# SSM tap angles as wrapping 32-bit integers on GpSimd, with sine and cosine read from integers, in a gated S4D and feed-forward kernel

## The chip, the cores and the metric

The kernel runs on one core of one Trainium2 chip. The metric is the device time of one execution in microseconds; 619.15 us is the median of two runs of the kernel before. In the profile the engines are PE (TensorE; PEld is its weight load), DVE (VectorE), ACT (ScalarE), POOL (GpSimd) and SP (SyncE, which issues the transfers).

## What is computed

An S4D state-space convolution over L = 2048 positions and D = 640 channels with N = 128 modes a channel, and a feed-forward layer with 1728 hidden units, both on tokens of the same shape, mixed by a gate:

```python
dt = jnp.exp(log_dt)
A = -jnp.exp(log_A_real) + 1j * A_imag
C = (C_real + 1j * C_imag) * dt[:, None]
P = jnp.exp((A * dt[:, None])[:, :, None] * pos[None, None, :])
K = 2.0 * jnp.einsum("dn,dnl->dl", C, P).real
...
y = jnp.fft.irfft(Uf * Kf[None, :, :], L2)[:, :, :L]
...
return g * a + (1 - g) * b
```

What matters here is `K`: for each channel 2048 taps, each a sum over 128 modes of an exponential times a cosine. The kernel writes a position as 32 times a coarse step (64 of them, numbered by `slots()`) plus a fine step (32 of them). By the addition theorem the taps of a channel are then a product of matrices over the modes: fine factors (128 x 32) against coarse factors (128 x 64). Each factor is a magnitude (exponential) times a sine or a cosine of an angle counted in turns.

## The kernel before

All of `f32` is multiplied on PE in the form `F32R`, large operands split in a high and a low part. The work has three strands.

*Feed-forward.* Three passes over the hidden units (`PARTS`), each over eight groups of 256 tokens. PE's products go to the tile `pf`: 512 columns for the first layer, 320 for the second. In the program this is the queue `ff`, with the best rank.

*Taps.* 40 steps of 16 channels; two steps make a pair. `params()` first turns the parameters, 128 channels by 640 on chip, into four quantities (the angle of a step `th`, the decay `la`, the start angle `ph`, the logarithm of the amplitude `mx`). `split` writes a high and a low part of each to memory (`ps`), and `load_rows` reads four steps of them back as `PS`, with one row for each of 16 channels, 4 quantities and 2 parts on the partitions. In each step `phases` multiplies these rows on PE by a constant, block-diagonal table `tg`: the result `pg` holds 1024 angles for each of 128 modes (16 channels, 32 fine and 32 coarse). ACT casts `pg` to whole turns (`cs`), DVE subtracts them (`sn`), and DVE clears the sign bit for the cosine (`cs`). `exponents` multiplies the same rows by other parts of `tg`: `px` (1024 coarse exponents) and `pe` (512 fine ones), and ACT takes `Exp` of both, into `mg` and `me`, and `Sin` of `sn` and `cs`. `factors` multiplies on DVE, in five instructions: `G` (two), `mg`, `cs`, `sn`. `taps` lets PE multiply the factors of a pair of steps into `pk` (128 small matmuls), DVE transposes `pk` into `kt`, POOL adds the skip term `dsk` to `kt`, and SP stores it (`kd`).

*Convolution.* When the last `kd` is under way, the taps' pools close and those of the convolution open (`start` in `conv`). Five blocks of 128 channels run through `stage1`, `stage2`, `inv2`, `relay` and `inv1`: PE's results go to `pc`, and DVE, ACT and POOL work on `ku`.

*Order.* `Plan` is a list scheduler that runs while the program is built. It has an estimate of each task's duration, a rank, and rings of buffers (`ring`), and gives each engine its instructions in one fixed order; on the chip each engine runs them in that order and waits on semaphores. A task that takes a slot of a ring waits until the users of an earlier tile are done. `taps` has a poorer rank on PE (`GTR`) than the feed-forward, so `pf` fills PE between the pairs; `phases` and `exponents` of a step are joined, so that `pg`, `px` and `pe` follow each other. All operations are recorded through one helper, so that one line number (L326) stands for all of them, and the tile names tell them apart.

Of the kernel before, what the change touches and what calls it, by code (L numbers as in the profile page):

```python
# [10 lines left out]
F32 = mybir.dt.float32  # L11
F32R = mybir.dt.float32r
# [7 lines left out]
NT = D // 128  # L20
# [46 lines left out]
TN = 0.7  # L67

# [10 lines left out]
def tables():  # L79
# [20 lines left out]
    tg = np.zeros((16, 8, 176))  # L100
    tg[:, :2, :32], tg[:, :2, 32:64], tg[:, 2:4, :32] = b, 32 * b + 16, 1
    tg[:, 4:6, 64:128], tg[:, 4:6, 128:160], tg[:, 6:, 128:160] = 32 * slots(), b, 1
    tg[np.arange(16), :, 160 + np.arange(16)] = 1
    f = lambda x: np.ascontiguousarray(x.astype(np.float32))
    return dict(t_g=f(tg.reshape(128, 176)), t_f1=f(np.tile(np.stack([f1, f1[slots()]], axis=1), (2, 1, 1))), t_w=f(w.reshape(128, 64)),
# [251 lines left out]
class Kernel:  # L357
    def __init__(self, tc, ctx, io, out):
# [7 lines left out]
        self.sc = dict(kd=T([NT, 4, 128, 16, 32], "kd"), ps=[T([1, 128, 8, 128], "ps0"), T([NT - 1, 128, 8, 128], "ps1")],  # L366
# [464 lines left out]
    def params(self):  # L831
# [5 lines left out]
        def step(eng, dur, fn, kb=0, ch='c', deps=()):  # L837
            last[ch] = [A(eng, 'prm' + ch, dur, fn, [*last[ch], *deps], kb=kb, rank=dict(a=PA, c=3, l=PL)[ch])]
            return last[ch][0]

        def start():
# [6 lines left out]
            for n in ("th", "ac", "as", "mx", "mn", "r", "s", "ph", "ra", "sa"):  # L848
                tl[n] = T(n)
            tl['ni'] = T("ni", I32)  # L850
        def start_c():
# [5 lines left out]
        last.update(a=[self.prm_load], c=[self.prm_load_c])  # L857

# [18 lines left out]
        self.rows_st = [], []  # L877

# [15 lines left out]
        split(0, 'th', 'a')  # L894
        steps(13, 0.68, lambda V: exp_(V, tl['la'], tl['ni'], tl['ra'], tl['sa']), 'a')
        ex = last['a']
        steps(NT, 0.2, scaled('la', 'la', -1.0), 'a')
        split(4, 'la', 'a')
# [35 lines left out]
        split(6, 'mx', 'l')  # L934
        for cond, two, turn in ((ALU.is_gt, True, 0.25), (ALU.is_lt, False, 0.5)):
# [8 lines left out]
        steps(3, 0.7, R(lambda V, ac, as_, cr, ci, mx, mn, r, s, ph, th, ni: (  # L944
            V.tensor_scalar(ni, th, 1008.0, None, op0=ALU.mult),
            V.scalar_tensor_tensor(r, th, 1008.0, ni, op0=ALU.mult, op1=ALU.subtract), V.tensor_add(ph, ph, r))), deps=ex)
        split(2, 'ph', 'c')
        done = [*last['a'], *last['c'], *last['l'], *self.rows_st[0], *self.rows_st[1]]
        self.tg_done = []


        def steps_in():
            tl['tgs'] = self.prm.tile([128, 176], F32, name="tgs")
            D_.dma_start(tl['tgs'], io['t_g'])

        def spread(ds):
            def go():
                a, b = self.tg[:, :2048].rearrange("p (x d j) -> p d x j", x=2, j=64), self.tg[:, 2048:].rearrange("p (d j) -> p d j", j=32)
                for d in ds:
                    m = tl['tgs'][:, 160 + d:161 + d]  # L960
                    S.mul(a[:, d], tl['tgs'][:, :128].rearrange("p (x j) -> p x j", x=2), m)
                    S.mul(b[:, d], tl['tgs'][:, 128:160], m)
            return go
        a = A('SP', 'tg', 0.62, steps_in, [self.prm0], kb=88, rank=TGR)
        if TGR > 5:
            self.late_loads.append(a)
        for d in range(0, 16, 2):
            self.tg_done.append(A('ACT', 'tg', 1.1, spread(range(d, d + 2)), [a], rank=TGA))
        return [*done, *self.tg_done]

    def ssm(self, C=16):
# [10 lines left out]
        self.tg = gk.tile([128, 2560], F32R, name="tg")  # L982
        dsk = gk.tile([128, n // 2, 2 * Q], F32, name="dsk")
        nc.gpsimd.memset(dsk, 0.0)
        for k, v in dict(pg=1, px=1, pk=1, sc=5, mg=4, G=2, kt=2, PS=2).items():
            ring(k, v)
# [18 lines left out]
        def load_rows(c):  # L1005
            r_ = tok('PS')

            def load():
                t = gk.tile([128, 4, 128], F32R, name="PS", bufs=2)
                src = self.sc['ps'][c >= 8][c // 8 - (c >= 8), c % 8 * C:c % 8 * C + 4 * C]  # L1010
                D_.dma_start(t.bitcast(F32), src.rearrange("(s p) k n -> (p k) s n", p=C))
                for k in range(4):
                    R[c + k] = t[:, k]
            a = A('SP', 'rows', 0.62, load, self.rows_st[c >= 8], take=[r_], kb=256, rank=1)
            for k in range(4):
                rows[c + k] = a, r_

        tasks, f = {}, {}
        I = lambda x: x.bitcast(I32)


        def phases(c):
            p_, s_ = tok('pg'), tok('sc')
            rd, r_ = rows[c]

            def pe():
                p = self.psg.tile([128, 4, 256], F32, name="pg")
                pf = p.rearrange("p d j -> p (d j)")
                st['pg'] = pf.rearrange("p (d j) -> p d j", j=64)
# [4 lines left out]
            def whole():  # L1034
                st['sc', c] = [st['gp'].tile([128, C, 64], F32, name=k, bufs=5) for k in ("sn", "cs")]
                S.copy(I(st['sc', c][1]), st['pg'])
# [474 lines left out]
```

## Time and profile before

| what | value |
|---|---|
| median of two runs | 619.15 us (617.43 to 620.88) |
| the profiled execution: span from first to last instruction | 615.6 us, 3.55 under the median |
| granted TensorE clock over the span | 1.000 |
| HBM | 67.79 MB read, 39.06 MB written |
| `pg` on PE, ACT, DVE (all matmuls, casts, subtractions) | 25.3, 40.4, 48.6 us busy |
| `px` on PE and ACT | 25.3, 41.2 us busy |
| table loads on ACT | 42, 53.9 us busy |

A row of a group reads: line, engine, operation, output and inputs by the program's names, shapes, count, then the busy time and the mean duration in ns, then the engine's idle time just before these instructions and who ended it. A row of a timeline or of the chain begins with its start and its duration in us. A row by stage has the stretch, its length, and for each engine the busy time and the number of instructions, then the granted clock, the share in which the DMA engines were busy, and GB/s. Matmuls are pipelined, so that their durations overlap; the distance between two starts is what one costs.

### The profile page before, as it was taken

To read this page: it belongs to the slowest core of one execution; us is meant where nothing else is said; L and a number is where in the kernel's file an instruction comes from. 1 tells how busy PE (TensorE), PEld (TensorE's weight loads), DVE (VectorE), ACT (ScalarE), POOL (GpSimd) and SP (SyncE) were. 2 spreads that over 40 slices of the span, in tenths; PEclk is the share of its full clock that TensorE was granted. 3 is DMA by queue.
4 is the path that set the end of the run, shared out by engine and by line. 5 is a ranking of instruction groups with operands and counts; after the bars stand their busy time and mean duration, and the time that the engine had idled before them with its cause. 6 is when DMAs were issued, how large, how long until landed. Compare 5 with 4: busy or idle time off the path is not lost.

```text
span 615.6 us, 18337 instructions
## 1 busy us (share of the span) xinstructions
PE 603.2 (98%) x7864; PEld 478.9 (78%) x7864; DVE 505.8 (82%) x794; ACT 399.2 (65%) x579; POOL 92.6 (15%) x134
## 2 busy tenths in 40 slices
PE   8999999999999999999999999999989999999996
PEld 6898988889879989989978988966565564755656
DVE  5998669999978999999999999866867796866942
ACT  6569269999898798887898989222235244352470
POOL 0000000000000000000000000002507062451744
PEclk9999999999999999999999999999999999999999
DMA  8993954624566435435331352768340836725244
GB/s 288 398 367 126 357 190 179 235 59 158 164 221 237 158 100 211 146 101 196 114 121 61 105 168 83 236 229 307 118 176 2 241 100 209 259 75 172 78 137 138
DMA packets 54474, 108.05 MB, mean 176 GB/s; under 512 B 5497, under 2 KB 30713, under 8 KB 53497
## 3 DMA queue, kind: packets, MB, share of 16 engines
q1 hardware_dynamic: 54168, 106.63, 51.1%
q8 instruction: 62, 1.02, 0.6%
q10 hardware_dynamic: 224, 0.25, 0.1%
q14 instruction: 20, 0.16, 0.1%
HBM read 67.79 MB, written 39.06 MB: 174 GB/s over the span
## 4 chain that ended last, share of the span: by engine, by line
PE 90%; DVE 3%; DMA 2%; ACT 2%; issue 1%; POOL 1%; ACTq 0%; DVEq 0%; POOLq 0%; SPq 0%
PE pf L326 59%; PE pc L326 18%; PE pk L326 6%; PE pg L326 3%; PE px L326 3%; PE pe L326 1%; DMA ws<-in_B_w_dram 1%; DVE G L326 1%; POOL q L326 1%; DVE ku L326 1%; DMA wq<-in_w_dram 1%; DMA kd<-kt 1%; DVE mg L326 0%; ACT L326 0%; DMA ws<-y__84 0%
## 5 line engine op out<-in xcount | busy, mean ns | idle before, releaser
L326 PE MATMUL pf<-xx,w1h 128*128 128x512 f32 x560 | 176.0, 402 | 1.2 <-DVE w1h L326 0.9
L326 PEld LDWEIGHTS pf<-xx,w1h 128*128 128x128 f32 x560 | 103.7, 190 | 36.6 <-issue 12.7
L326 PE MATMUL pf<-xx,w1l 128*128 128x512 f32 x260 | 102.2, 393 | 0.0
L326 ACT COPY ku<-pc 128x512 f32<-128x512 f32 (+1 forms) x60 | 44.1, 758 | 81.7 <-PE pc L326 55.9
L326 DVE STREAM_TRANSPOSE ku<-pc 128x512 f32<-128x512 f32 x80 | 50.4, 685 | 23.3 <-PE pc L326 23.2
L326 POOL TENSOR_TENSOR kt<-kt,dsk 128x8 f32<-128x8 f32 x20 | 9.0, 451 | 394.9 <-DVE kt L326 341.2
L326 POOL TENSOR_TENSOR ku<-ku 128x256 f32<-128x256 f32 x80 | 56.4, 742 | 69.5 <-DVE ku L326 49.3
L326 PE MATMUL pf<-w2h,hh 128*128 128x320 f32 x192 | 59.3, 313 | 0.8 <-DVE q L326 0.8
L326 PE MATMUL pf<-w2l,hwh 128*128 128x320 f32 x192 | 59.2, 309 | 0.0
L326 PE MATMUL pf<-w2h,hwh 128*128 128x320 f32 x192 | 59.1, 309 | 0.0
L326 PE MATMUL pf<-w2h,hwl 128*128 128x320 f32 x192 | 56.9, 310 | 1.8 <-DVE hwl L326 1.8
L326 PE MATMUL pf<-w2l,hh 128*128 128x320 f32 x192 | 58.5, 309 | 0.0
L326 PEld LDWEIGHTS pf<-xx,w1l 128*128 128x128 f32 x260 | 49.0, 189 | 10.9 <-DVE w1l L326 0.2
L326 DVE TENSOR_TENSOR ku<-pc,ku 128x512 f32<-128x512 f32 x80 | 52.5, 682 | 4.2 <-ACT ku L326 2.9
L326 ACT CAST cs<-pg 128x1024 int32<-128x1024 f32 x40 | 40.4, 1010 | 21.7 <-PE pg L326 21.4
L326 ACT ACT_TABLE_LOAD x42 | 53.9, 1283 | 0.8
L326 DVE TENSOR_TENSOR sn<-pg,cs 128x1024 f32<-128x1024 f32 x40 | 48.6, 1214 | 2.3 <-ACT cs L326 2.3
L326 DVE TENSOR_TENSOR mg<-mg,cs 128x1024 f32<-128x1024 f32 x40 | 48.9, 1221 | 1.7 <-ACT cs L326 0.2
L326 PE MATMUL pf<-w2h,hl 128*128 128x320 f32 x160 | 48.0, 316 | 0.0
L326 ACT ACTIVATE cs<-cs,half_pi 128x1024 f32<-128x1024 f32 x40 | 45.6, 1140 | 0.0
L326 PE MATMUL pc<-ku,tm 64*32 64x256 f32 x1280 | 42.6, 392 | 0.5 <-issue 0.2
L326 ACT ACTIVATE sn<-sn 128x1024 f32<-128x1024 f32 x40 | 42.2, 1055 | 0.2
(151 smaller groups left out, 1250.7 us busy)
## 6 DMA issues: line engine op xcount, KB each, us to landing
xx<-xt SPq DMA_DIRECT2D x24, 640.0 KB, 5.6
xt<-xx SPq DMA_DIRECT2D x16, 640.0 KB, 7.2
part<-q SPq DMA_DIRECT2D x16, 640.0 KB, 3.1
q<-part SPq DMA_DIRECT2D x16, 640.0 KB, 4.4
xl<-in_u_r_dram SPq DMA_DIRECT2D x16, 320.0 KB, 4.3
xu<-in_u_b_dram SPq DMA_DIRECT2D x5, 1024.0 KB, 6.2
kd<-kt SPq DMA_DIRECT2D x80, 64.0 KB, 1.8
xu<-in_x_t_dram SPq DMA_DIRECT2D x6, 640.0 KB, 6.0
```

Source lines behind the costliest of these rows:

```text
L326: self._last = self._tc.keep_in_program_order(f(*a, **k))
```

## The change

*Angles.* The angles are no longer products on PE. `params()` takes, on DVE, the fractions of a turn of 16 angles and of one angle of a step (`fraction`), transposes them, the decay and the start angle on PE (`across`: five 128x128 transposes each, into `tr`), and lets ACT write them, times 2^32, as 32-bit integers into `cn` (the decay stays f32). Four POOL instructions of 640 columns make the cosine's and the odd-multiple variants. `cn` goes to memory and comes back for four steps at a time as `cn`, with the modes on the partitions. In each step POOL makes `ca` (1024 integers: the counts of a channel times odd numbers), `ck` (512: the counts times 0 to 31) and `fa` (1024: `ck` plus the start angle); sums and products wrap at 32 bits, which takes away whole turns. ACT reads `ca` and `fa` as integers into `Sin` with the scale 2 pi / 2^32, in place.

*Exponents.* `px` is gone: DVE multiplies the decay in `cn` by a row of 64 slot numbers `td` into `mg`, and ACT takes `Exp` of it from SBUF. `pe` stays, one matmul, with half of the rows (two quantities) and a table `tg` of 1024 columns for two steps.

*Factors.* Four DVE instructions instead of five: the two fine products become one of 1024 columns, on `fa`.

*Around it.* `tg` is spread from its small form by two POOL instructions instead of 32 on ACT; of the splits two are left (decay, amplitude). The rings `pg`, `px` and `sc` go; `ca` (4 slots), `fa` (7) and `tm` (2, the buffer of `ck`) come. The first reading of `ck` by the convolution waits for the last angle step, since the buffer is shared.

```diff
+    odd = 2 * b + 1
+    ti = np.concatenate([odd, np.where(b % 2, -odd, odd), b, [1 << 30]]).astype(np.int32)
...
+        def across(k, src, ch, deps=()):
...
+                for t in range(NT):
+                    self.E.transpose(tl['tr', k][:, t], tl[src][:, t], self.ident)
...
+                if k == 5:
+                    S.copy(o.bitcast(F32), x)
+                else:
+                    S.mul(o, x, 2.0 ** 32)
...
+        def fraction(to, src, k, n='ni'):
...
+                V.tensor_scalar(i, x, k, None, op0=ALU.mult)
+                V.scalar_tensor_tensor(o, x, k, i, op0=ALU.mult, op1=ALU.subtract)
...
-                for h in range(2):
-                    x = slice(h * 512, h * 512 + 512)
-                    self.E.matmul(pf[:, x], R[c], self.tg[:, x], start=True, stop=True)
...
-                S.copy(I(st['sc', c][1]), st['pg'])
...
-            d = A('DVE', 'g1', 1.14, lambda: V.tensor_sub(st['sc', c][0], st['pg'], I(st['sc', c][1])), [b],
-                  use=[p_, s_], rank=G1R)
-            e = A('DVE', 'g1', 0.62, lambda: V.tensor_scalar(I(st['sc', c][1]), I(st['sc', c][0]), 0x7fffffff, None,
-                                                             op0=ALU.bitwise_and), [d], use=[s_], rank=G1R, port=True)
...
+            def coarse():
+                t = st['ca', c] = st['gp'].tile([128, C, 2, 32], F32, name="ca", bufs=CA)
+                P.tensor_tensor(t.bitcast(I32), two(0), self.ti[:, None, :64].rearrange("p o (s j) -> p o s j", s=2).to_broadcast([128, C, 2, 32]),
+                                op=ALU.mult)
...
+                P.tensor_tensor(st['tm', c], X[c][:, 4, :, None].to_broadcast([128, C, 32]),
+                                self.ti[:, None, 64:96].to_broadcast([128, C, 32]), op=ALU.mult)
...
+                P.tensor_tensor(t.bitcast(I32), st.pop(('tm', c))[:, :, None].to_broadcast([128, C, 2, 32]), two(2), op=ALU.add)
...
+                    S.activation(x, x.bitcast(I32), AF.Sin, scale=TWO_PI / 2 ** 32)
...
-                    self.E.matmul(pf[:, x], R[c], self.tg[:, 1024 + h * 512:1536 + h * 512], start=True, stop=True)
...
+                V.tensor_mul(t, X[c][:, 5, :, None].bitcast(F32).to_broadcast([128, C, 64]),
+                             self.td[:, None].to_broadcast([128, C, 64]))
...
-                    elif k == 3:
-                        V.tensor_mul(cs[:, :, :32], me, cs[:, :, :32])
                     else:
-                        (P if POOLED else V).tensor_mul(sn[:, :, :32], me, sn[:, :, :32])
+                        V.tensor_mul(st['fa', c], st['me', c][:, :, None].to_broadcast([128, C, 2, 32]), st['fa', c])
```

The order of the instructions moves with it. POOL in the tap stage, before: all of the skip sums of the 20 pairs stand in a row, with the convolution's first sums behind them.

```order
L326 TENSOR_TENSOR kt<-kt,dsk 128x8 x20
L326 TENSOR_TENSOR ku<-ku 128x256 x32
L326 TENSOR_TENSOR yo<-yo,yj 128x512
L326 TENSOR_TENSOR yo<-yo,yj 128x256
L326 TENSOR_TENSOR q<-q,ws 128x128 x2
```

After, a stretch of the same stage: the skip sum of a pair, then the angle instructions of the next two steps, and so on for all pairs.

```order
L329 TENSOR_TENSOR kt<-kt,dsk 128x8
L329 TENSOR_TENSOR ca<-cn,ti 128x1024
L329 TENSOR_TENSOR ck<-cn,ti 128x512
L329 TENSOR_TENSOR fa<-ck,cn 128x1024
L329 TENSOR_TENSOR ca<-cn,ti 128x1024
L329 TENSOR_TENSOR ck<-cn,ti 128x512
L329 TENSOR_TENSOR fa<-ck,cn 128x1024
L329 TENSOR_TENSOR kt<-kt,dsk 128x8
```

So POOL's stage of 20 small instructions becomes one of 140, and a skip sum stands behind the angles of two steps.

DVE in the same stage, before, for one step and the beginning of the next (`q` is the feed-forward's running sum, `xl` the gate's product):

```order
L326 TENSOR_TENSOR sn<-pg,cs 128x1024
L326 TENSOR_SCALAR cs<-sn 128x1024
L326 SCALAR_TENSOR_TENSOR G<-mg,sn 128x16x32
L326 TENSOR_TENSOR G<-mg,sn 128x16x32
L326 TENSOR_TENSOR mg<-mg,cs 128x1024
L326 TENSOR_TENSOR q<-pf,q 128x320
L326 TENSOR_TENSOR cs<-me,cs 128x16x32
L326 TENSOR_TENSOR sn<-me,sn 128x16x32
```

After, for a step:

```order
L329 STREAM_TRANSPOSE kt<-pk 128x8x2x32
L329 TENSOR_TENSOR mg<-cn,td 128x1024
L329 TENSOR_TENSOR q<-pf,q 128x320
L329 TENSOR_TENSOR mg<-cn,td 128x1024
L329 SCALAR_TENSOR_TENSOR G<-mg,ca 128x16x32
L329 TENSOR_TENSOR G<-mg,ca 128x16x32
L329 TENSOR_TENSOR mg<-mg,ca 128x1024
L329 TENSOR_TENSOR fa<-me,fa 128x1024
```

The pair of `sn` and `cs` with its input from PSUM (`pg`) is gone, and the product of the exponents stands ahead of the factors that use it.

PE at the end of the tap stage, before: behind the last `pk` the first matmuls of the convolution (`pc`) stand between matmuls of the feed-forward (`pf`).

```order
L326 MATMUL pk<-G,sn 32x64 x4
...
L326 MATMUL pc<-ck,tf 64x512 x8
L326 MATMUL pf<-xx,w1h_4198 128x512 x2
L326 MATMUL pf<-xx,w1l_4199 128x512
L326 MATMUL pc<-xu,tf 64x512 x12
L326 MATMUL pf<-xx,w1h_4225 128x512 x2
L326 MATMUL pf<-xx,w1l_4226 128x512
```

After, there are seven `pf` and then the convolution's first block without any:

```order
L329 MATMUL pk<-G,fa 32x64 x4
...
L329 MATMUL pf<-w2h_4211,w2l_5195 128x320
L329 MATMUL pc<-ck,tf 64x512 x8
L329 MATMUL pc<-xu,tf 64x512 x16
L329 MATMUL pc<-ck,tf 64x512 x8
L329 MATMUL pc<-ku,tm 32x256 x128
L329 MATMUL pc<-ck,tf 64x512 x4
```

Behind the last `pk` there were 156 `pf` of 512 columns and 288 of 320; now there are 60 and 127. The others have moved ahead of it, into the room that `pg` and `px` took.

More of the change, by code (lines that the diff above doesn't have):

```diff
@@ L942, in params @@
             V.tensor_scalar(mn, mn, -2.0, 1.0, op0=ALU.mult, op1=ALU.add), V.tensor_mul(ph, ph, mn))))
[L944 to L968, printed above, removed]
+        across(2, 'ph', 'c', deps=last['t'])
+        self.cn_st = []
+        for k, gs in enumerate((slice(0, 2), slice(2, 2 * NT))):
+            self.cn_st.append(A('SP', 'prm', 0.62, lambda k=k, gs=gs: D_.dma_start(self.sc['cn'][k].bitcast(I32), tl['cn'][:, gs]),
+                                list(turned), kb=196 * (gs.stop - gs.start), rank=1))
+        done = [*last['a'], *last['c'], *last['l'], *self.rows_st[0], *self.rows_st[1], *self.cn_st]
         return [*done, *self.tg_done]
@@ L1006, in load_rows @@
             r_ = tok('PS')
+            k = c >= 8
             def load():
[L1009 to L1019, printed above, removed]
-        def phases(c):
-            p_, s_ = tok('pg'), tok('sc')
+                t, x = gk.tile([128, 2, 128], F32R, name="PS", bufs=2), gk.tile([128, 6, 64], I32, name="cn", bufs=2)
+                src = self.sc['ps'][k][c // 8 - k, c % 8 * C:c % 8 * C + 4 * C]
+                D_.dma_start(t.bitcast(F32), src.rearrange("(s p) k n -> (p k) s n", p=2 * C))
+                D_.dma_start(x, self.sc['cn'][k].bitcast(I32)[:, c // 4 - 2 * k])
```

171 lines of the change are left out of this document (105 added, 66 removed).

## The prediction

> **What bounds the kernel now.** I read the page's busy shares first, then the busy time by stage, then the chain of waits, then the instruction groups of each engine in the middle stage, and last the POOL timeline set beside the DVE timeline. The first two views:
>
> ```profile
> span 615.6 us, 18337 instructions
> PE 603.2 (98%) x7864; PEld 478.9 (78%) x7864; DVE 505.8 (82%) x794; ACT 399.2 (65%) x579; POOL 92.6 (15%) x134
> ...
> core 0: us, PE busy (x) PEld busy (x) DVE busy (x) ACT busy (x) POOL busy (x), PEclk, DMA share, GB/s
> ...
> 84.20:404.20 320.00, 317.70 (x4042) 280.05 (x4040) 296.54 (x440) 271.49 (x317) 8.80 (x19) 1.00 0.45 150
> 404.20:615.60 211.40, 204.54 (x3408) 127.33 (x3404) 145.03 (x236) 78.27 (x161) 82.94 (x108) 1.00 0.49 161
> ```
>
> PE is busy for 98% of the span, so the sum of PE's work sets the end. But the middle stage, in which the taps are made, has DVE at 296.5 of 320 us and ACT at 271.5 too, while POOL does 8.8 us. The chain shows where that stage begins and ends:
>
> ```profile
> 84.67 1.01 ACT cs L326
> ...
> 402.30 1.92 PE pk L326 x128
> 404.22 4.30 PE pf L326 x18
> 408.52 1.88 PE pc L326 x16
> ```
>
> The convolution (`pc`) begins only behind the last `pk`: its pools open when the last taps are out. So there are two ways to lose or win: PE work saved, and the time at which the last `pk` can run. One step (16 channels, 40 of them) takes 320/40 = 8.0 us now.
>
> **PE, saved and added.** The rows of one visit, a group for a 128x128 f32 pass, and the first and last of a run of 29 matmuls of 320 columns:
>
> ```profile
> 136.46 0.62 PE L326 MATMUL pg<-tg,PS 128*128 128x512 f32 x2
> 136.92 0.62 PE L326 MATMUL px<-tg,PS 128*128 128x512 f32 x2
> 137.38 0.40 PE L326 MATMUL pe<-tg,PS 128*128 128x512 f32 x1
> ...
> L326 PE MATMUL pe<-ident 128*128 128x128 f32 x12 | 2.9, 434 | 1.5 <-POOL ident masks.py:199 1.5
> ...
> 145.00 0.30 PE L326 MATMUL pf<-w2h,hh 128*128 128x320 f32 x1
> ...
> 149.09 0.30 PE L326 MATMUL pf<-w2h,hh 128*128 128x320 f32 x1
> ```
>
> Starts are what count on a pipelined engine: four matmuls from 136.46 to 137.38 are 0.23 us each. The change removes the two of `pg` and the two of `px` in each step: 160 x 0.23 = 36.8 us of PE. It adds 20 transposes (4 of 5). Their price is not in the trace: by columns it would be 0.23/4 = 0.06, as two of the 0.24 us passes (2.9/12) it would be 0.48. I take 0.23 each, one such pass, the middle of ends that lie 8 us apart in all: 4.6 us, between 1.2 and 9.7. Net 32 us off PE.
>
> **DVE, for each step.** The groups of the middle stage:
>
> ```profile
> L326 DVE TENSOR_TENSOR mg<-mg,cs 128x1024 f32<-128x1024 f32 x40 | 48.9, 1221 | 1.7 <-ACT cs L326 0.2
> L326 DVE TENSOR_TENSOR sn<-pg,cs 128x1024 f32<-128x1024 f32 x40 | 48.6, 1214 | 2.3 <-ACT cs L326 2.3
> L326 DVE TENSOR_SCALAR cs<-sn 128x1024 int32<-128x1024 int32 x40 | 27.5, 687 | 0.9
> L326 DVE TENSOR_TENSOR G<-mg,sn 128x512 f32<-128x512 f32 x40 | 27.4, 684 | 0.0
> L326 DVE TENSOR_TENSOR sn<-me,sn 128x512 f32<-128x512 f32 x40 | 27.3, 682 | 0.0
> L326 DVE TENSOR_TENSOR cs<-me,cs 128x512 f32<-128x512 f32 x40 | 27.3, 682 | 0.0
> L326 DVE SCALAR_TENSOR_TENSOR G<-mg,sn 128x512 f32<-128x512 f32 x40 | 27.0, 675 | 4.0 <-ACT sn L326 4.0
> ...
> L326 DVE SCALAR_TENSOR_TENSOR xl<-xl,gw 128x640 f32<-128x640 f32 x14 | 11.5, 821 | 4.3 <-DMA xl<-in_u_r_dram 4.3
> ...
> L326 DVE TENSOR_TENSOR w1l<-ws,w1h 128x640 fp32r<-128x640 f32 x9 | 7.1, 812 | 0.0
> L326 DVE TENSOR_TENSOR w2l<-ws,w2h 128x640 fp32r<-128x640 f32 x9 | 7.1, 818 | 0.0
> ```
>
> A step costs 1.221 + 1.214 + 0.687 + 0.684 + 0.682 + 0.682 + 0.675 = 5.85 us now. Gone are the subtraction (1.214), the mask (0.687) and two products (1.364); new are `mg<-cn,td` and `fa<-me,fa`, both 1024 columns, 1.22 each by the `mg<-mg,cs` row. That leaves 1.22 x 3 + 0.684 + 0.675 = 5.02 us, 0.83 less. Alone, DVE would need 296.5 - 33 = 263.5 us for the stage, 6.6 a step. But every one of the five that are left reads two tensors from SBUF; the biggest one removed read one of its two from PSUM.
>
> **ACT.** It loses the cast, and its two sines stay two of 1024 columns, now read as int32. The rows show no price for that type, since the cast to int32 takes no longer than a sine in f32:
>
> ```profile
> L326 ACT ACTIVATE sn<-sn 128x1024 f32<-128x1024 f32 x40 | 42.2, 1055 | 0.2
> L326 ACT CAST cs<-pg 128x1024 int32<-128x1024 f32 x40 | 40.4, 1010 | 21.7 <-PE pg L326 21.4 <-ACT hwh L326 0.2
> ```
>
> So 1.01 us a step goes, and the 32 small spreads of `tg`. ACT has 48 us to spare in the stage already, so the gain is costed at nothing; if the cover went, 1.06 a sine would still fit into 8 us.
>
> **POOL, the new work.** The nearest rows are plain f32 sums:
>
> ```profile
> L326 POOL TENSOR_TENSOR ku<-ku 128x256 f32<-128x256 f32 x80 | 56.4, 742 | 69.5 <-DVE ku L326 49.3 <-issue 20.1
> L326 POOL TENSOR_TENSOR yo<-yo,yj 128x512 f32<-128x512 f32 x8 | 10.1, 1282 | 15.3 <-ACT yo L326 15.3
> ```
>
> The slope is (1282 - 742)/256 = 2.11 ns a column, so 1024 columns are 1282 + 512 x 2.11 = 2.36 us. A step is two of 1024 and one of 512: 2.36 x 2 + 1.28 = 6.0 us, 240 us over the stage. That int32 products cost what f32 sums cost is a choice: no row shows a POOL product, and no row of another engine shows int32 dearer than f32 (0.687 for 1024 int32 columns on DVE is cheaper than any two-input form). The floor is this 6.0.
>
> **The two engines together.** Here is what decides. POOL's small `kt` sums (8 columns, 20 of them) beside what DVE did at that moment, DVE rows second:
>
> ```profile
> 223.60 0.21 POOL L326 TENSOR_TENSOR kt<-kt,dsk 128x8 f32<-128x8 f32 x1 [12.87 <-DVE kt L326]
> 223.44 1.19 DVE L326 TENSOR_TENSOR sn<-pg,cs 128x1024 f32<-128x1024 f32 x1
> ...
> 210.16 0.57 POOL L326 TENSOR_TENSOR kt<-kt,dsk 128x8 f32<-128x8 f32 x1 [15.76 <-DVE kt L326]
> 210.00 0.65 DVE L326 SCALAR_TENSOR_TENSOR G<-mg,sn 128x512 f32<-128x512 f32 x1
> 210.57 0.70 DVE L326 TENSOR_TENSOR G<-mg,sn 128x512 f32<-128x512 f32 x1
> ...
> 141.17 0.70 POOL L326 TENSOR_TENSOR kt<-kt,dsk 128x8 f32<-128x8 f32 x1 [16.41 <-DVE kt L326]
> 141.01 0.78 DVE L326 TENSOR_TENSOR w1l<-ws,w1h 128x640 fp32r<-128x640 f32 x1
> ```
>
> The sum takes 0.21 us while DVE reads from PSUM (`sn<-pg,cs`), though DVE is busy all that time. It takes 0.57 while DVE runs `G`, and 0.70 while DVE runs `w1l<-ws,w1h`; both times it ends 0.08 us behind DVE's instruction (210.65 and 210.73; 141.79 and 141.87). I went through all 20: thirteen are long, and each of them stands against a DVE instruction with two SBUF inputs, or one with a single SBUF input in the fast form (`cs<-sn`); the seven short ones stand against PSUM reads or an idle DVE. So POOL does not run beside such an instruction; it waits for its end.
>
> The trace shows this one way round. Whether DVE waits as long for a POOL instruction of 2.4 us no row shows: all long POOL work of the kernel before lies in the convolution, where DVE reads PSUM. I bound it from both sides. If DVE never waits and POOL, once started, is not held up: DVE needs 6.6 us a step, POOL 6.0, PE more than either, and contention costs nothing. If the two exclude each other: a step needs DVE's 5.02, POOL's 6.0, and 1/40 of the stage's other DVE instructions with two SBUF inputs, (11.5 + 7.1 + 7.1)/40 = 0.64: 11.66 us. With DVE instructions overlapping at their ends by 0.08 (210.57 against 210.65 above), about eight a step, it is 11.06; with no DVE work under POOL's at all it is 6.6 + 6.0 = 12.6. I take exclusion, 11.66, because it is nearest to the thirteen rows: a wait to the end of the instruction is what they show, not a slower pace.
>
> A rule of the Trainium skill goes further than the row (SBUF — State Buffer, section on SBUF's two separate sides): the pair of ports that GpSimd shares with VectorE is an exclusive lock, taken for the whole instruction by whichever starts first, and a VectorE instruction with two SBUF inputs takes it against a GpSimd one that reads SBUF. The trace agrees with that rule where POOL waits (0.57 against 0.21 us); the other way round no run here shows it yet. By the rule a step is the 11.66 us above; without it, the 6.6.
>
> **The rest of the order.** The parameter stage loses three DVE steps and two splits, and gains four transposes with their copies, four POOL sums of 640 columns and the spread of `tg` on POOL; they lie under `pf`, and by the same exclusion some of POOL's ten us can delay DVE's parameter chain. On SP, two `rows` loads take the place of each one, and two `cn` stores the place of two `ps` pairs; all are small beside their lead. What is queued behind the new waits: PE runs in written order, so while it waits for the factors of a `pk` the `pf` behind it wait too, and a late step is lost time, not filled time. The `kt` sum now stands behind POOL's angle work, up to 6 us late; that costs once, at the last pair, where nothing of it is left to run. I let the stage begin at 88 instead of 84.2 (4.6 for the transposes, part hidden); none and 7 are the ends. If PE's `pf` no longer hide gaps, it is in the convolution: of `pf` behind the last `pk` there are 156 of 512 columns and 288 of 320 in the order before, 60 and 127 after, so 0.23 x 156 + 0.147 x 288 = 78.2 us become 32.5 (0.147 = 4.09/28 from the rows above), and the first pass of the convolution has hardly a filler. The last stage was 211.4, so 211.4 - 45.7 = 166 with the same gaps; I add 8 for lost cover (0 to 16): 174.
>
> **Sum.** 88 + 40 x 11.66 + 174 = 728 us. The profiled execution's span of 615.6 stands 3.55 under the median of 619.15, so 732 us.
>
> **Rivals.**
> - *No contention worth the name.* PE stays the bound: between the first `pe` and the last `pk` the new order has 562 `pf` of 512 columns and 961 of 320, 270.5 us by the prices above; with 40 x 0.23 for `pe` and 20 x 2.0 for `pk` (1.92 and a turn) it is 320 us, and 88 + 320 + 174 = 582. By PE's sum it is 615.6 - 32 = 583.6 plus lost cover. Time: 588, between 585 and 602. For it: no row shows DVE waiting for POOL. Against it: thirteen of thirteen.
> - *Partial exclusion.* If DVE loses a share x of POOL's 6.0 us, a step is 6.6 + 6.0x. The kernel gets no faster where 88 + 40T + 174 = 615.6, T = 8.84, x = 0.37; within 2% is x from 0.32 to 0.43. Above that it is slower: 632 to 700 us for x from 0.43 to 0.71.
>
> Two rows bear on the third, of one shape and two operations:
>
> ```profile
> L326 DVE RECIPROCAL s<-mx 128x128 f32<-128x128 f32 x5 | 4.6, 936 | 0.0
> ...
> L326 DVE TENSOR_SCALAR th<-ld_a 128x128 f32<-128x128 f32 x5 | 1.1, 284 | 0.0
> ```
>
> - *Products of int32 are slow on POOL.* The furthest that rows of one shape lie apart by their operation is on DVE, 936 against 284 ns, a factor of 3.3; with it a step is (2.36 + 1.28) x 3.3 + 2.36 = 14.4 us of POOL alone, and the time 88 + 576 + 174 + 3.55 = 842.
>
> **How the numbers follow.** Full exclusion 0.58 (700 to 777 us by its bounds: 88 + 442 + 166 and 88 + 504 + 182, each with 3.55), partial and slower 0.10, slow products 0.04, about the same 0.05, no contention 0.23. So slower 0.72, same 0.05, faster 0.23; two per cent is about what a measurement of this kernel can tell from no change. The likeliest case's own range is 700 to 777; the range that holds eight in ten reaches over the partial cases to the faster one: 585 to 777.
>
> **What would show it.** Right: POOL `ca`, `ck`, `fa` with mean spans well over 2.36 and 1.28 us, or DVE rows of `G` and `mg` well over 0.68 and 1.22 us; PE waiting for DVE in front of `pk`; the last `pk` past 530 us. Wrong: the last `pk` near 410 with PE busy throughout, which would mean the two engines read side by side; or a step near 14 us with DVE idle, which would mean slow products.

## The result, and the profile after

The changed kernel takes 733.88 us (median of two runs, 731.08 to 736.69) where the kernel before takes 619.15: a ratio of 1.185, with a 95% interval of 1.172 to 1.199. It is slower, as forecast (732 us). The head of its page:

```profile
span 734.4 us, 18068 instructions
PE 611.4 (83%) x7724; PEld 472.1 (64%) x7724; DVE 612.1 (83%) x713; ACT 355.7 (48%) x509; POOL 373.9 (51%) x260
```

PE fell from 98% to 83%, and no engine is over 83%: by shares alone nothing bounds this kernel. The busy time by stage says more. The cuts are the first `pe` and the end of the last `pk`; the columns are those of the prediction's rows by stage.

```profile
0.00:91.70 91.70, 85.44 (x454) 74.35 (x455) 68.56 (x123) 43.39 (x72) 11.04 (x14) 1.00 0.81 295
91.70:517.88 426.18, 352.63 (x4125) 304.71 (x4124) 408.64 (x374) 240.31 (x288) 280.77 (x139) 0.94 0.40 130
517.88:734.43 216.56, 173.28 (x3147) 93.06 (x3147) 134.92 (x217) 72.05 (x150) 82.14 (x108) 0.92 0.40 125
```

The tap stage grew from 320 to 426 us, and there DVE is busy for 408.6 us, 96%, with 66 instructions fewer than before (374 against 440). In the last stage PE is busy for 31 us less (204.5 before, 173.3 now), and the stage still takes 216.6 us, 5 more than before. Both are to be explained. The instruction groups of DVE and POOL that the prediction spoke of:

```profile
L329 POOL TENSOR_TENSOR ca<-cn,ti 128x1024 int32<-128x1024 int32 x40 | 100.5, 2513 | 117.6 <-DVE mg L329 72.3 <-issue 17.6 <-DMA PS<-ps 13.8
L329 POOL TENSOR_TENSOR fa<-ck,cn 128x1024 int32<-128x1024 int32 x40 | 93.8, 2345 | 3.1
L329 POOL TENSOR_TENSOR ck<-cn,ti 128x512 int32<-128x512 int32 x40 | 69.4, 1735 | 0.0
...
L329 DVE TENSOR_TENSOR fa<-me,fa 128x1024 f32<-128x1024 f32 x40 | 70.5, 1763 | 0.0
L329 DVE TENSOR_TENSOR mg<-mg,ca 128x1024 f32<-128x1024 f32 x40 | 66.4, 1659 | 0.9
L329 DVE TENSOR_TENSOR mg<-cn,td 128x1024 f32<-128x1024 f32 x40 | 62.4, 1582 | 0.0
L329 DVE SCALAR_TENSOR_TENSOR G<-mg,ca 128x512 f32<-128x512 f32 x40 | 49.7, 1242 | 0.0
L329 DVE TENSOR_TENSOR G<-mg,ca 128x512 f32<-128x512 f32 x40 | 45.4, 1136 | 0.0
```

`mg<-mg,ca` was 1.22 us in the same shape before and is 1.66 now, `G` was 0.68 and is 1.14 to 1.24. What is in the longer spans shows in the timeline, POOL's rows first and DVE's behind them (start, duration):

```profile
304.90 2.83 POOL L329 TENSOR_TENSOR ca<-cn,ti 128x1024 int32<-128x1024 int32 x1 [4.28 <-DVE mg L329]
307.70 1.50 POOL L329 TENSOR_TENSOR ck<-cn,ti 128x512 int32<-128x512 int32 x1
309.28 2.32 POOL L329 TENSOR_TENSOR fa<-ck,cn 128x1024 int32<-128x1024 int32 x1
...
304.68 1.22 DVE L329 TENSOR_TENSOR fa<-me,fa 128x1024 f32<-128x1024 f32 x1
...
306.65 1.64 DVE L329 SCALAR_TENSOR_TENSOR G<-mg,ca 128x512 f32<-128x512 f32 x1
308.21 0.68 DVE L329 SCALAR_TENSOR_TENSOR hwl<-pf,hwh 128x512 fp32r<-128x512 f32 x1
308.81 0.94 DVE L329 TENSOR_TENSOR G<-mg,ca 128x512 f32<-128x512 f32 x1
309.78 2.90 DVE L329 TENSOR_TENSOR mg<-mg,ca 128x1024 f32<-128x1024 f32 x1
```

The two take turns. `ca` starts while `fa<-me,fa` runs (to 305.90) and ends 1.83 us behind it, at 307.73. `G` starts at 306.65, while `ca` runs, and ends at 308.29: 0.56 us behind `ca`, less than its own 0.68. `mg` starts at 309.78, waits out `fa` (to 311.60) and ends at 312.68. Between them `hwl`, which reads one input from PSUM, takes its usual 0.68 us beside POOL's `ck`. So DVE's busy 408.6 us is in good part waiting (e1_few below puts a number on it), and a wait of this sort is counted as busy.

PE's waits in the tap stage (who waited for whom, us in total, times, longest):

```profile
PE pk L329 <- DVE fa L329: 34.5, 18, 7.6
PE pe L329 <- ACT me L329: 10.7, 7, 4.0
PE pf L329 <- DVE hwl L329: 10.4, 6, 3.9
```

The longest is the one announced: `pk` waits for the last factor of its pair, and since PE runs in written order, the `pf` behind it wait too.

### The profile page after: what moved, and what is told of

The parts are those of the page before. It is cut to its first block, busy times and chain, and to the rows that moved or that the text cites. A ratio compares the mean times of both kernels' runs of the same rounds, so it can differ in the third digit from the quotient of the medians.

```text
span 734.4 us, 18068 instructions
## 1 busy us (share of the span) xinstructions
PE 611.4 (83%) x7724; PEld 472.1 (64%) x7724; DVE 612.1 (83%) x713; ACT 355.7 (48%) x509; POOL 373.9 (51%) x260
## 5 line engine op out<-in xcount | busy, mean ns | idle before, releaser
L329 POOL TENSOR_TENSOR ca<-cn,ti 128x1024 int32<-128x1024 int32 x40 | 100.5, 2513 | 117.6 <-DVE mg L329 72.3
L329 POOL TENSOR_TENSOR fa<-ck,cn 128x1024 int32<-128x1024 int32 x40 | 93.8, 2345 | 3.1
L329 ACT ACTIVATE mg<-mg 128x1024 f32<-128x1024 f32 x40 | 42.4, 1060 | 86.0 <-DVE mg L329 83.9
L329 PE MATMUL pk<-mg,fa 128*32 128x64 f32 x1280 | 47.2, 234 | 34.5 <-DVE fa L329 34.5
L329 PE MATMUL pf<-w2h,hh 128*128 128x320 f32 x192 | 63.0, 332 | 14.6 <-DVE q L329 13.2
L329 DVE TENSOR_TENSOR fa<-me,fa 128x1024 f32<-128x1024 f32 x40 | 70.5, 1763 | 0.0
L329 POOL TENSOR_TENSOR ck<-cn,ti 128x512 int32<-128x512 int32 x40 | 69.4, 1735 | 0.0
L329 PEld LDWEIGHTS pk<-mg,fa 128*32 128x32 f32 x1280 | 40.1, 119 | 42.6 <-DVE fa L329 37.6
L329 DVE TENSOR_TENSOR mg<-mg,ca 128x1024 f32<-128x1024 f32 x40 | 66.4, 1659 | 0.9
L329 DVE TENSOR_TENSOR mg<-cn,td 128x1024 f32<-128x1024 f32 x40 | 62.4, 1582 | 0.0
```

The source lines that it names most:

```text
L329: self._last = self._tc.keep_in_program_order(f(*a, **k))
```

## The experiments

Two theories. *Exclusion*: a POOL instruction and a DVE instruction with two SBUF inputs do not run side by side, in either order, and that is where the tap stage's 107 us went. *Elastic filler*, formed from the last stage above: the convolution runs at its own pace, and `pf` there only fills PE's waits, so `pf` moved ahead of it saves nothing. The rivals are in the expectations. All edits are against the changed kernel unless said otherwise. A table of the cuts first, worked out from the rows by stage (us). The median is over all runs of a version; the stages are those of its profiled execution, and the expectations speak of that execution's span, the sum of the three stages:

| run | median | start | tap stage | DVE, POOL busy in it | last stage | PE busy in it, clock |
|---|---|---|---|---|---|---|
| before | 619.15 | 84.9 | 319.4 | 296.5, 8.8 | 211.3 | 204.5, 1.00 |
| after | 733.88 | 91.7 | 426.2 | 408.6, 280.8 | 216.6 | 173.3, 0.92 |
| e1_few | 638.08 | 92.5 | 330.5 | 279.2, 82.5 | 214.6 | 171.9, 0.92 |
| e2_ca_twice | 790.68 | 92.8 | 486.3 | 470.5, 388.6 | 209.9 | 170.3, 0.94 |
| e4_me_psum | 703.10 | 92.1 | 399.0 | 366.6, 249.8 | 209.9 | 168.5, 0.94 |
| e5_mg_psum | 699.57 | 92.6 | 390.6 | 373.4, 279.0 | 210.9 | 167.9, 0.94 |
| e7_few_plan | 625.00 | 92.4 | 307.0 | 273.6, 94.8 | 224.2 | 196.9, 0.95 |
| e9a_all_psum | 645.85 | 92.1 | 342.4 | 299.9, 214.0 | 209.3 | 169.8, 0.94 |
| e9f_f32 (one run) | 639.37 | 91.8 | 335.3 | 295.7, 208.4 | 210.0 | 169.8, 0.93 |
| e11_angles_only | 658.17 | 96.0 | 333.9 | 281.2, 242.6 | 227.2 | 216.6, 0.98 |
| e12_angles_free | 647.39 | 96.1 | 331.6 | 247.2, 214.1 | 218.7 | 202.1, 0.97 |
| e13_full_rows | 629.16 | 91.4 | 317.8 | 248.6, 213.6 | 218.9 | 202.5, 0.97 |

**e1_few: POOL's work cut to a sixteenth.**

```diff
-                P.tensor_tensor(t.bitcast(I32), two(0), self.ti[:, None, :64].rearrange("p o (s j) -> p o s j", s=2).to_broadcast([128, C, 2, 32]),
-                                op=ALU.mult)
+                t = st['cas', c] = st['gp'].tile([128, 1, 2, 32], F32, name="cas", bufs=3)
+                P.tensor_tensor(t.bitcast(I32), two(0)[:, :1], self.ti[:, None, :64].rearrange("p o (s j) -> p o s j", s=2), op=ALU.mult)
...
-                    S.activation(x, x.bitcast(I32), AF.Sin, scale=TWO_PI / 2 ** 32)
+                    x = st[k, c] = st['gp'].tile([128, C, 2, 32], F32, name=k, bufs=CA if k == 'ca' else FA)
+                    y = st.pop((k + 's', c)).bitcast(I32).to_broadcast([128, C, 2, 32])
```

> The three POOL instructions of a step make only the angles of one channel in sixteen (64, 32 and 64 columns instead of 1024, 512 and 1024) and the sines read those sixteen times over; the other angles are left out. Everything else, and the order, is as after the change. If POOL's work is what stretches the tap stage, DVE needs its own 6.6 us a step, PE is the bound again, and the stage from the first pe to the last pk falls from 427 us to 320-340; with the last stage as it is (217), the span falls from 734 to 627-650, not below the 615.6 of before. If the order (fewer pf left where they hide waits) is what costs, the tap stage stays over 400 and the span over 700. If the lost cover in the convolution is a consequence of POOL's delays and not of the order, the last stage falls too, to about 174, and the span is about 585.

The tap stage fell by 95.7 us to 330.5, as the first of the three says; the last stage stayed at 214.6, so the third is refuted. With the same DVE instructions, DVE's busy time fell by 129.4 us (408.64 to 279.19), which is the least that DVE had spent waiting for POOL. And the ratio to the kernel before is still 1.030 (1.026 to 1.035): in this order the change would not have been faster without the load on POOL either.

**e2_ca_twice: one more instruction for POOL.**

```diff
+                P.tensor_tensor(t.bitcast(I32), two(0), self.ti[:, None, :64].rearrange("p o (s j) -> p o s j", s=2).to_broadcast([128, C, 2, 32]),
+                                op=ALU.mult)
```

> The product that makes ca is run twice into the same tile in each step: 40 more POOL instructions of 1024 integers; all else as after the change. Under mutual exclusion of POOL with DVE's two-SBUF-input instructions each one adds what POOL needs by itself, 1.8 to 2.0 us: 72-80 us in the tap stage, a span of 806-814. If POOL's time only counts through its busy share, there is room: it is busy for 282 of the stage's 427 us, so 40 x 2.0 = 80 us more fit in beside DVE, and the span stays within 734 +/- 12.

The tap stage grew by 60.1 us, 1.50 for each added instruction, and DVE's busy time in it by 61.9. POOL's idle third did not take them in. The size is under the 1.8 to 2.0 expected, and the span of 789.0 under 806. By the 2.02 us that `ca` takes in e9a_all_psum below, about a quarter of an added instruction would lie beside DVE work that does not exclude it; that quarter was not measured by itself.

**e4_me_psum and e5_mg_psum: one input from PSUM.** e4 moves the fine decay, e5 the coarse one.

```diff
-                        st['me', c] = st['gp'].tile([128, C, 32], F32, name="me", bufs=4)
-                        S.activation(st['me', c], st.pop(('pe', c)), AF.Exp)
+                        st['me', c] = st.pop(('pe', c))
+                        S.activation(st['me', c], st['me', c], AF.Exp)
```

```diff
-                t = st['mg', c] = st['gp'].tile([128, C, 64], F32, name="mg", bufs=4)
+                t = st['mx', c] = self.psg.tile([128, C, 64], F32, name="tr", bufs=2)
...
-                        V.tensor_mul(m, m, ca[:, :, None, 1].to_broadcast([128, C, 2, 32]))
+                        st['mg', c] = st['gp'].tile([128, C, 64], F32, name="mg", bufs=4)
+                        V.tensor_mul(o, m, ca[:, :, None, 1].to_broadcast([128, C, 2, 32]))
```

> The fine decay me stays in PSUM (Exp in place on pe, two banks), so that the product fa<-me,fa reads one input from PSUM and one from SBUF; all POOL work and all DVE work is as after the change. If two SBUF inputs are what excludes, fa<-me,fa falls from 1.76 to 1.22 us mean and 40 x 1.22 = 49 us go: a span of 680-695. If both engines only share SBUF's rate, or DVE loses to POOL whatever it reads, fa<-me,fa stays near 1.7 and the span within 734 +/- 12.

> The coarse decay stays in PSUM until its last use (mg<-cn,td writes PSUM, Exp in place there, and G, G and mg read it from there; the product goes to SBUF for the tap matmuls); POOL's and DVE's operations and sizes are as after the change. If two SBUF inputs are what excludes, 2.58 us a step leave the exclusion: what is left in it is 1.22 + 1.22 + 0.64 of DVE and 4.4 of POOL, 7.5 us, under PE's 8.0, so the tap stage falls from 427 to 320-345 us and the span to 625-655; G falls from 1.14-1.24 to about 0.7 us and mg<-mg,ca from 1.66 to about 1.2. If the engines share SBUF's rate whatever DVE reads, the rows and the span stay as they are, 734 +/- 12.

Both are faster than the change, but by 31 and 34 us by their medians: the spans of 701.0 and 694.0 lie outside the ranges of 680 to 695 and 625 to 655. The rows that were moved did what exclusion says; of e4 and of e5:

```profile
L329 DVE TENSOR_TENSOR fa<-pe,fa 128x1024 f32<-128x1024 f32 x40 | 48.5, 1213 | 0.0
```

```profile
L329 DVE TENSOR_TENSOR mg<-tr,ca 128x1024 f32<-128x1024 f32 x40 | 48.3, 1208 | 0.0
L329 DVE TENSOR_TENSOR G<-tr,ca 128x512 f32<-128x512 f32 x40 | 27.0, 674 | 0.0
L329 DVE SCALAR_TENSOR_TENSOR G<-tr,ca 128x512 f32<-128x512 f32 x40 | 26.8, 671 | 4.4 <-ACT ca L329 4.4
...
L329 DVE TENSOR_TENSOR tr<-cn,td 128x1024 f32<-128x1024 f32 x40 | 101.1, 2527 | 0.0
```

1.21 and 0.67 us, the prices without any load. But `tr<-cn,td`, which still reads two SBUF tensors, went from 1.58 to 2.53 us. POOL's three instructions stand back to back, and one DVE instruction that meets them waits out the one that runs: in e5 a `tr<-cn,td` starts at 303.25 us, while `ca` runs (303.07 to 305.05), takes 2.89 us and ends 1.09 us behind `ca`. The waits do not shrink in step with the number of DVE instructions that can wait; the sum of both engines' times is no good price for a part of the exclusion. The buffers differ too: `me` had four slots in SBUF and has the two of `pe` in e4, and PE waits 28.8 us there ahead of `pe` for the product that frees a slot; e5 has two slots for the coarse decay instead of four. So the two misses are not the exclusion's alone, and their shares were not separated.

**e9a_all_psum: no DVE instruction of a step with two SBUF inputs.** `me` as in e4, `mg` in one PSUM slot, and the slot numbers in PSUM:

```diff
-        self.ti, self.td = gk.tile([128, 97], I32, name="ti"), gk.tile([128, 64], F32, name="td")
+        self.ti, self.td = gk.tile([128, 97], I32, name="ti"), self.psg.tile([128, 64], F32, name="td")
...
-            ks = [(c - 2, 3), (c - 2, 4), (c - 1, 3), (c - 1, 4), (c, 1), (c, 2), (c + 1, 1), (c + 1, 2)]
+            ks = [(c, 3), (c, 4), (c + 1, 3), (c + 1, 4), (c, 1), (c, 2), (c + 1, 1), (c + 1, 2)]
```

> None of DVE's five instructions of a step reads two tensors from SBUF any more: the slot numbers td, the coarse decay (one slot of two banks) and the fine decay (Exp in place in pe) are in PSUM; the sines of a pair stand ahead of its exponentials on ACT, G has 4 buffers, and the planner has POOL at 2.0 and 1.05 us. POOL's work is that of the change, at full size. If exclusion by two SBUF inputs is the whole cause, DVE's rows come down to 1.22 and 0.68 us, POOL's ca and fa to their own 1.9-2.05 and ck to 0.9-1.1, and the tap stage to the 325-345 of a kernel without POOL's load (e1_few: 330): a span of 628-650. If POOL's load holds the stage in another way as well (its rings, its chain to the sines, or SBUF's rate), the tap stage stays over 370 and the span over 675.

This is what exclusion says: a span of 643.7 us (median 645.85), the tap stage at 342.4, DVE's five rows at 1.21 to 1.22 and 0.68 us, and all of POOL's work still there (its `fa` a little over the 1.9 to 2.05 expected):

```profile
L329 POOL TENSOR_TENSOR fa<-ck,cn 128x1024 int32<-128x1024 int32 x40 | 86.7, 2167 | 3.1
L329 POOL TENSOR_TENSOR ca<-cn,ti 128x1024 int32<-128x1024 int32 x40 | 80.6, 2015 | 89.5 <-DVE mg L329 49.0 <-issue 15.7 <-DMA cn<-cn 14.1
L329 DVE TENSOR_TENSOR tr<-cn,td 128x1024 f32<-128x1024 f32 x40 | 48.7, 1217 | 0.0
...
L329 POOL TENSOR_TENSOR ck<-cn,ti 128x512 int32<-128x512 int32 x40 | 43.8, 1096 | 0.0
```

That none of DVE's five rows of a step is longer beside POOL's full work is what shows the cause. How much of the 88 us between the medians comes from the four buffers of `G`, the order of the sines and the planner's shorter POOL times, which came with this edit, was not separated.

This run also gives POOL's own price for a step: 2.015 + 1.096 + 2.167 = 5.28 us, where the prediction had 6.0. The rule of the Trainium skill that the prediction set beside its rows (SBUF — State Buffer, section on SBUF's two separate sides: whichever of the two starts first holds the shared ports for its whole instruction, and the other is blocked) was shown there only for POOL; by the `G` and `mg` of the timeline above, 1.64 and 2.90 us for 0.68 and 1.22, and by this run, the trace agrees with it for DVE too.

**e9f_f32: the type.** As e9a_all_psum with f32 tensors.

> As e9a_all_psum, with POOL's three instructions on f32 numbers of the same shapes instead of int32 (the angles that come out are not those of the reference, so this part of the computation is left out). It prices the type where nothing holds POOL up. If a POOL instruction of 1024 columns costs what my slope over the f32 sums of the kernel before says, the products and sums in f32 take 2.36 us where the int32 ones take 2.0, and int32 is the cheaper form; if the type costs nothing, both take the same within 3 per cent, and the slope was wrong for this shape. The span stays that of e9a_all_psum within 10 us.

```profile
L329 POOL TENSOR_TENSOR fa<-ck,cn 128x1024 f32<-128x1024 f32 x40 | 84.4, 2111 | 3.1
L329 POOL TENSOR_TENSOR ca<-cn,tg 128x1024 f32<-128x1024 f32 x40 | 77.4, 1934 | 89.8 <-DVE mg L329 50.6 <-issue 16.0 <-DMA PS<-ps 13.6
```

1.93 us for the f32 product, 2.02 for int32: 4%, just past the 3 I had set, and the sum differs less (2.11 and 2.17). So the type was hardly a term; the slope was too steep for the long shape. The span of 637.1 is that of e9a_all_psum within 7 us.

**e7_few_plan: the same work, with `pf` kept for the convolution.** As e1_few, and

```diff
-            a = A('POOL', 'gp', 2.4, coarse, [rd, opened], take=[c_], use=[r_], rank=G1R)
+            a = A('POOL', 'gp', 0.7, coarse, [rd, opened], take=[c_], use=[r_], rank=G1R)
```

> As e1_few (angles of one channel in sixteen made, the others left out), but the planner is given POOL's shorter times (0.7, 0.42 and 0.6 us for ca, ck and fa instead of 2.4, 1.3 and 2.4), so that it lets the taps run earlier and leaves 60 us of pf behind the last pk, by its own count, where e1_few leaves 32. The work on each engine is the same. Theory: the last stage is set by the convolution's own chain of about 211 us, and pf only fills its gaps. Then the tap stage falls from 330 to 300-308 us, the last stage stays at 207-217, and the span falls from 637.6 to 603-617. Rival, the sum of my prediction: the end is set by the amount of PE work, so what leaves the tap stage comes back behind it: the last stage grows by the same 28 us, and the span stays at 630-645.

The span is 623.6 us, between the two. The tap stage fell by 23.5 us, as the theory says, and the last stage grew by 9.6, which neither says. PE's busy time there grew by 25.0 us, so some 60% of the PE work put behind the last `pk` was free. The other direction is plainer: the seven runs with 180 to 187 `pf` behind the last `pk` (after, e1, e2, e4, e5, e9a, e9f) take 209 to 217 us for the last stage, and the kernel before takes 211 with 444. But the stage is not wholly free of `pf`: in the versions below, e12 and e13 take 219 us with 417, and e11 takes 227 with 480.

**e11, e12, e13: the angles alone.** These put the coarse exponents back on PE, into PSUM. e11 leaves `fa<-me,fa` with two SBUF inputs; e12 keeps `me` in PSUM too; e13 is e12 with tables of 128 rows instead of 64, and, beside that, with 5 buffers of `fa` instead of 7 and its larger table spread on ACT.

```diff
-                V.tensor_mul(t, X[c][:, 5, :, None].bitcast(F32).to_broadcast([128, C, 64]),
-                             self.td[:, None].to_broadcast([128, C, 64]))
+                    self.E.matmul(t.rearrange("p d j -> p (d j)")[:, h * 512:h * 512 + 512], R[c][r],
+                                  self.tgx[r, h * 512:h * 512 + 512], start=True, stop=True)
```

> Only the angles of the change: the coarse exponents are a product on PE again (two matmuls of 512 columns with 64 rows, into PSUM, Exp in place there), G, G and mg read the decay from PSUM, and fa<-me,fa is the one instruction of a step that reads two SBUF tensors; POOL's angle work is that of the change. DVE's own work is 3.80 + 1.6 = 5.4 us a step, and its waits for POOL, at 0.54 for fa and about 0.8 for the 0.9 xl and weight splits, about 1.3: 6.7 us, under PE's pace. PE has 18.4 us less than the kernel before and 18.4 more than the change. The planner leaves 85 us of pf behind the last pk. If the last stage is the convolution's own 211 us with pf as filler, the span is 92 + 295 to 305 + 211 to 218 = 598-615, at or below the kernel before. If the amount of PE work sets the end, it is 615.6 - 18.4 + 4 = 601, which does not tell the two apart by itself, but then the last stage must be over 220. If one locked instruction a step is enough to hold the stage, it is over 640.

> The angles of the change without the exclusion: the coarse exponents are a product on PE (two matmuls of 512 columns, 64 rows) into one PSUM slot, the fine decay stays in pe (two banks), G has 4 buffers, and no DVE instruction of a step reads two SBUF tensors. DVE's own work is 3.8 + 1.6 us a step, POOL's 5.3, neither the pace. The planner leaves 72 us of pf behind the last pk, near the 78 of the kernel before. PE has 18.4 us less than the kernel before and about 4 more for transposes. If the exclusion and the thin last stage are the two places where the change loses, the tap stage is 300-315 us, the last one 211-222, and with a start of 92-96 the span is 603-625: the same as before within 2 per cent, and near 115 us under the change. In e11_angles_only one locked instruction a step was left; if what held its tap stage at 334 was not that one but POOL's work or the matmuls of 64 rows, the stage stays at 325-335 here and the span is over 635.

> As e12_angles_free, but the two tables of the exponents span all 128 rows again (1024 and 2048 columns) so that pe and tr are matmuls of 128x128 like pf; the tables' larger one is spread on ACT. In e12_angles_free PE was busy for 327.4 of the tap stage's 331.6 us at full clock, and each visit of a matmul with 64 rows cost about 0.35 us more than its columns (pe 0.43 and the pf behind it 0.26, where 0.23 and 0.147 are usual). If that is the price, 80 visits give back 24-32 us of PE: a tap stage of 298-312, and a span of 612-628, within 2 per cent of the kernel before. If PE's sum has another part that I have not found, the tap stage stays over 320 and the span over 636.

e11 and e12 missed their first forecasts, with tap stages of 334 and 332 us; the spans of 657.1 and 646.4 are those of the last case that each expectation names. In e12 DVE is at 247 us and PE at 327.4 of the stage: PE is the bound, and not through its columns. Around a matmul with 64 rows:

```profile
300.49 0.30 PE L329 MATMUL pf<-w2h,hwl 128*128 128x320 f32 x1
300.72 0.49 PE L329 MATMUL pe<-tg,PS 64*128 64x512 f32 x1
301.14 0.32 PE L329 MATMUL pk<-mg,fa 128*32 128x64 f32 x8
```

`pe` takes 0.42 us from start to start, where four such matmuls of 128 rows in the kernel before took 0.23 each, and the start before it lies 0.23 back instead of 0.147. The step to `pk` changes the shape too, and costs 0.32 behind a `pe` of 128 rows; but where `pf` follows, the medians over the stage are 0.43 in e12 and 0.23 in e13, and from a `pf` of 320 columns to `pe` 0.24 and 0.15. That is what a change of the tile's shape costs here. The Trainium skill has a rule that would account for it (TensorEngine Tiling (Array Packing), Key Properties: a change of the tiling mode drains the engine); the trace agrees with it in this extra. With 128 rows, e13, PE's busy time in the stage fell by 20.4 us and the stage by 13.8, to 317.8: less than the 24 to 32 expected, and above the 298 to 312 for the stage. e13 takes 629.16 us, 1.013 times the kernel before (1.009 to 1.017): the best of the versions that do all the work, within 2% of the kernel before and not faster. No version that I made beats the kernel before.

## Why the prediction was right, and where it was not

The sum of 728 us came within 6.4 of the span, but by two errors of opposite sign: the tap stage was put 40 us too long and the last stage 43 us too short. That the total came out so close is luck; the mechanism of the tap stage is not.

*The start.* 88 us forecast, 91.7 measured, 6.8 more than before: the transposes take 2.9 us of PE where 4.6 was put, and PE waits 3.3 us for DVE's fractions ahead of two groups of them, a wait that the sum did not have.

*The mechanism of a step.* Right: exclusion, both ways. The timeline shows the waits of either engine, e1_few and e2_ca_twice that POOL's load sets the length of the stage, and e9a_all_psum that DVE's two SBUF inputs are the condition.

*The size of a step.* 11.66 us forecast, 426.2/40 = 10.65 measured, 40 us in all. The term that was mis-sized is POOL's 6.0: the slope over 256 and 512 columns was carried to 1024, and e9a_all_psum measures 5.28. With it the sum is 5.02 + 5.28 + 0.64 = 10.94, and the 0.29 that is left lies within the overlap at the ends that made my lower bound (0.6 a step). By itself a step of 10.65 would also fit partial exclusion, with x = 0.68; what decides is the rows, in which each wait lasts to the end of the other engine's instruction.

*The last stage.* 174 us forecast, 216.6 measured. The step that failed is "211.4 - 45.7 = 166 with the same gaps": the gaps did not stay the same. PE's busy 204.5 of 211.3 us looked like a bound, and much of it was filling. The convolution's own matmuls in this stage, before and after (the row by stage for `pc` alone, without a column for POOL):

```profile
404.20:615.60 211.40, 120.53 (x2960) 57.27 (x2960) 102.87 (x160) 64.88 (x140) 1.00 0.49 161
517.70:734.40 216.70, 133.44 (x2960) 60.20 (x2960) 101.86 (x160) 65.48 (x140) 0.92 0.40 125
```

`pf` went from 89.8 us busy to 42.5, 47 us less. Against that, the same 2960 matmuls of `pc` are busy for 12.9 us more, at a granted clock of 0.92 instead of 1.00, and PE's idle time grew by 36.5 us, from 6.8 to 43.3. Three waits make 27.8 us of the 43.3:

```profile
PE pc L329 <- DVE ku L329: 13.9, 24, 5.2
PE pc L329 <- DMA ck<-kd: 8.2, 1, 8.2
PE pf L329 <- DVE q L329: 5.7, 1, 5.7
```

So the idle time came back where `pf` had stood. I had 8 us for lost cover on top of 166, and it was 51. That the convolution's own chain would take its 211 us with any amount of `pf` is the theory that fits the seven runs; it was not shown apart from the slower clock, and e7_few_plan and e11 to e13 keep to it only in part.

*The announced signs.* DVE's rows of `G` and `mg`, POOL's `ck` (1.74 us against 1.28) and PE's wait ahead of `pk` came as announced. POOL's other two did not: `ca` is only a little over 2.36 us (2.51) and `fa` under it (2.35), because the price itself was too high. The last `pk` past 530 us did not: it ended at 517.9, because the step was over-sized.

*The rivals.* "No contention" was priced at 588 us, through the same last stage of 174. e1_few, the run nearest to that case, takes 638, with a tap stage of 330.5 us for the 320 of the sum and a last stage of 214.6. So the rival that would have made the change faster was mispriced by 50 us, and the chance of 0.23 for faster stood on a sum that no run without POOL's load came near: with more `pf` kept for the convolution, e7_few_plan takes 625.0, about the time of the kernel before. Slow int32 products are refuted by e9f_f32, where f32 takes about as long.

*What stays open.* Why e7_few_plan's last stage grew by 9.6 us with 25 us more PE work in it, when the kernel before hides 78 us of `pf` there; the order of `pf` differs, and so does the granted clock (below). For the same reason it stays open how much of the last stage's 51 us the clock took, and how much the waits. Nor did any run separate, in e11_angles_only, the one locked instruction from the 64 rows; e12_angles_free, with none of a step locked, has a tap stage only 2 us shorter.

## What to carry to other kernels

Before work moves to POOL, count what DVE does beside it with two SBUF inputs: the wait hides in both engines' busy time, and no share of the page shows it, only a group whose mean grew with its shape unchanged. Leaving one operand in PSUM, where the engine before it can put it, takes that instruction's wait away (1.66 to 1.76 us became 1.21 here), but while others of the same step still read two tensors from SBUF, much of the time goes into their waits: 31 and 34 us came back with a part of them moved, 88 with all. And before PE work is saved, ask of each stage whether PE's busy share there is its pace or its filling: take the filler out, and see whether the stage gets shorter.

## What was not expected of the hardware

The granted TensorE clock was 1.000 over the whole kernel before, and 0.944 after. It falls where PE waits. Three stretches around the 8.24 us that the convolution waits for a load of `ck`, columns as by stage (the clock is the number ahead of the DMA share):

```profile
517.90:526.00 8.10, 6.97 (x55) 2.42 (x55) 6.48 (x11) 0.00 (x0) 0.21 (x1) 1.00 0.67 186
526.00:534.00 8.00, 0.07 (x4) 0.10 (x7) 1.65 (x3) 0.00 (x0) 0.00 (x0) 0.78 0.97 344
534.00:538.00 4.00, 3.54 (x16) 0.79 (x16) 1.71 (x3) 0.00 (x0) 0.00 (x0) 0.58 0.39 155
```

The clock is 1.00 ahead of the wait, and 0.58 in the 4 us behind it, when PE has work again. Two groups of sixteen matmuls of one shape, on the same tiles, from the timeline of PE, the first ahead of the wait and the second behind it (duration in the second column):

```profile
518.99 1.95 PE L329 MATMUL pc<-ck,tf 64*64 64x512 f32 x16
533.93 3.62 PE L329 MATMUL pc<-ck,tf 64*64 64x512 f32 x16 [8.24 <-DMA ck<-kd]
```

So this wait of PE cost more than its length: 1.7 us more for the next sixteen. Over the profiled runs the last stage's clock goes roughly with PE's share in it: 0.92 to 0.94 at 80 to 81% (the seven runs with little `pf`), 0.95 at 88% (e7_few_plan), 0.97 at 92 to 93% (e12, e13), 0.98 at 95% (e11), 1.00 at 97% (before). The two are not independent, since slower matmuls keep PE busy longer. How much of the last stage this takes was not measured by itself; the 12.9 us more for the same `pc` are what shows of it in PE's busy time.
